# Attention rows stored by token and gathered by the experts, instead of scattered into expert order

## The chip, the cores and the metric

The kernel runs on one core of a Trainium2 chip. The metric is the device time of one execution in microseconds (us); the median of three runs stands for the kernel. A profile is one further execution, with the hardware profiler on.

## The reference

Sliding-window attention with a distance bias feeds a top-1 mixture of experts. All is float32.

```python
# attention: B, H, S, D = 8, 8, 576, 64; window 128
scores = scale * q @ k.T + bias[h]            # bias: -slope(h) * distance
mask   = (rel >= 0) & (rel < 128)
attn   = softmax(where(mask, scores, -1e9))
x      = (attn @ v) as (B*S, H*D)              # N = 4608 tokens, 512 wide
# experts: E = 8, F = 1024
logits     = x @ w_gate                        # (N, 8)
expert_idx = argmax(logits, axis=1)
gate_w     = softmax(logits)[expert_idx]
y[n]       = relu(x[n] @ w1[expert_idx[n]]) @ w2[expert_idx[n]]
out        = gate_w[:, None] * y
```

## The kernel before

**Attention stage.** The work is 32 units `u`: 8 sequences `b` times 4 pairs of heads `hp`. The order of instructions on each engine is written by hand (`manual_schedule`), so each engine executes in the order in which the Python code issues. One turn of the main loop (lines 902 to 949) issues `scores(u)` (TensorE, L641, with the exponentials on ScalarE, L648), `values(u - 1)` (TensorE, L674, then copies L681 and L682 on ScalarE and an addition L683 on VectorE), `factors(u)` (VectorE multiplies the exponentials by a table, L654 and L659), `totals(u - 1)` (TensorE, L695), and then a share of the routing of the sequence before.

**Routing.** A sequence is four token tiles of 128 rows (even `b`) or five (odd `b`). Its routing is spread over four turns of the loop:

1. `logits_t` and `fold`: gate products and softmax denominators (L755, L716).
2. `gate` and `pick`: the logits per token and the chosen expert (L775 to L182).
3. `place` (two products with 0/1 matrices, L194 and L195, then L198, L203, L204 on VectorE, which give `slots`, each token's row number in expert order), `gate_exps`, and `row` for tiles 0 and 1 (four transposes, L806, and a multiplication on VectorE, L809, which makes the row `xs`).
4. `row` for the remaining two or three tiles, then `gate_weights` (L792, L793).

Turn four also queues the tiles as `unsent`; `send()` (L816) then lets GpSimd copy token number and gate weight into the row (L822) and scatter 128 rows of 528 floats with one indirect DMA (L138) into `x_rows`, a DRAM tensor with a region of N rows per expert. Two or three tiles are sent per turn.

**Buffers of PSUM.** Seven kinds of intermediate share one pool, `ps_m`, with three buffers under the one name `m`, handed out in turn: two for each `values`, two for `logits_t`, one for `fold`, one or two for `gate`, one for `place`, one for each `row`. A request waits until whoever reads the tile three requests back has finished with it.

**Between the stages.** `last_tasks` (L857) routes the last sequence and runs layer 1 of the first two tiles of expert 0 (the `early` group, read at L853 from the rows of the first six sequences). Rows that no token filled are cleared by scatters of a zero row (`clear`, L147), after `number_all_free` (L214) found them. `extras` (L405) lists the tiles beyond four per expert.

**Expert stage.** Each expert has a full group of four tiles, computed by seven half-size products instead of eight (`seven1`, `seven2`, products at L1048); after each expert but the first there is a group of one further tile (L507, L518). `gather` (L1144) clears free rows and loads the group's rows with plain DMAs of SyncE (L1151); `turn` transposes them (L498); `tokens` (L476) takes token numbers and gate weights out of the rows; `send_out` (L465) scatters results to `out` from GpSimd. Weights of an expert (w1 and w2, 2 MB each) are loaded one group ahead into two buffers each (L239, L246).

Of the kernel before, what the change touches and what calls it, by code (L numbers as in the profile page):

```python
# [15 lines left out]
P = 128  # L16
# [5 lines left out]
def kernel(  # L22
# [81 lines left out]
    tok_i = iota("tok", [P, NT], [[P, NT]], 0, 1, whole=True)  # L104

# [12 lines left out]
    x_d = nc.dram_tensor("x_rows", (E * N, RW), F32, kind="Internal").ap()  # L118
    x_tok = nc.dram_tensor("x_by_token", (NT, P, RW), F32, kind="Internal").ap()
    zero_row = consts.tile([P, RW], F32, name="zero_row")  # L120
    soon.append(lambda: nc.gpsimd.memset(zero_row[:], 0.0))
    soon.append(lambda: nc.gpsimd.memset(zero_row.bitcast(I32)[:, Dm : Dm + 1], 2 * N))


    EJ = 2
    free_rows = rte.tile([P, E, NJ], I32, name="free_rows")
    early_free = rte.tile([P, EJ], I32, name="early_free")
    late_free = rte.tile([P, EJ], I32, name="late_free")

    def number_free(out, tmp, count, tail, start, end):  # L130

        nc.vector.tensor_tensor(tmp, count, tail, op=ALU.add)
        nc.vector.tensor_scalar(out, tmp, scalar1=float(end), scalar2=float(E * N), op0=ALU.is_ge, op1=ALU.mult)
        nc.vector.tensor_tensor(tmp, tmp, out, op=ALU.add)
        nc.vector.tensor_tensor(out, tmp, start, op=ALU.add)

    def to_x_rows(row, numbers, apart=True):
        ins = nc.gpsimd.indirect_dma_start(  # L138
            out=x_d[:, :], out_offset=bass.IndirectOffsetOnAxis(ap=numbers, axis=0),
            in_=row, in_offset=None, bounds_check=E * N - 1, oob_is_err=False,  # L140
        )
        ins = getattr(ins, "ins", ins)
        if apart:
            tc.declare_no_dep(ins, group="rows_in", reason="disjoint rows")
            tc.add_to_no_dep_group("rows_in", ins)

    def clear(rows, apart=True):  # L147
        for j in range(rows.shape[1]):
            to_x_rows(zero_row[:], rows[:, j : j + 1], apart)
# [37 lines left out]
    def place(tiles, tmp_pool, ps, name):  # L187
# [17 lines left out]
        if tiles[-1] == NT - 1:  # L205
            nc.vector.tensor_sub(cnt[:], rk[:, :, GT], region[:])
        elif t0 + n == early_end:
            nc.vector.tensor_copy(early_n[:], rk[:, 0, GT:])
            number_free(
                early_free[:], tmp_pool.tile([P, EJ], F32, name="free", bufs=1)[:], early_n[:].to_broadcast([P, EJ]),  # L210
                tail[:, :EJ], region[:, 0:1].to_broadcast([P, EJ]), EJ * P,
            )

    def number_all_free(tmp_pool):  # L214

        tmp = tmp_pool.tile([P, E, NJ], F32, name="free", bufs=1)
        late = tmp_pool.tile([P, 1], F32, name="late", bufs=1)
        nc.vector.tensor_scalar_max(late[:], cnt[:, 0:1], float(EJ * P))
        number_free(
            late_free[:], tmp[:, 0, :EJ], late[:].to_broadcast([P, EJ]), tail[:, :EJ],  # L220
            region[:, 0:1].to_broadcast([P, EJ]), CAP,
        )
        number_free(
            free_rows[:], tmp[:], cnt[:].unsqueeze(2).to_broadcast([P, E, NJ]),
            tail[:, None, :].to_broadcast([P, E, NJ]), region[:].unsqueeze(2).to_broadcast([P, E, NJ]), CAP,
        )

    def scatter(t, row):
        to_x_rows(row, slots[:, t : t + 1])
# [26 lines left out]
    def shifted():  # L256
        with tc.tile_pool(name="bias", bufs=1) as b_pool, \
# [44 lines left out]
            for t in range(NT):  # L302
# [83 lines left out]
                nc.vector.tensor_copy(xs.bitcast(I32)[:, Dm : Dm + 1], tok_i[:, t : t + 1])  # L386
                nc.vector.reciprocal(xs[:, Dm + 1 : Dm + 2], gw[:])
                nc.sync.dma_start(x_tok[t], xs[:])
# [87 lines left out]
    def tokens(g):  # L476

        n = g["n"]
        bits = g["xg"].bitcast(I32)[:, :n, Dm]
        si = plain.tile([P, NJ], I32, name="si", bufs=2)  # L480
        g["si"], g["gw"] = si, plain.tile([P, NJ], F32, name="gw", bufs=2)
        if "mask" in g:
            nc.vector.tensor_tensor(si[:, :n], bits, g["mask"][:, 0, :], op=ALU.bitwise_and)
            nc.vector.tensor_tensor(si[:, :n], si[:, :n], g["mask"][:, 1, :], op=ALU.bitwise_or)
        else:
            nc.vector.tensor_copy(si[:, :n], bits)
        nc.vector.tensor_copy(g["gw"][:, :n], g["xg"][:, :n, Dm + 1])
# [66 lines left out]
    with tc.tile_pool(name="tab", bufs=1) as tab, \  # L554
# [50 lines left out]
        later.append(lambda: nc.vector.tensor_copy(ends.bitcast(I32)[:, :, 0], tok_i[:]))  # L605
# [184 lines left out]
        def gate_weights(ts):  # L790
            tt = slice(ts[0], ts[-1] + 1)
            nc.vector.tensor_scalar_add(gsum[:, tt], gsum[:, tt], 1e-9)  # L792
            nc.vector.reciprocal(ends[:, tt, 1], gsum[:, tt])  # L793
# [21 lines left out]

        def send():  # L816
            ts, i = unsent.pop(0)
            t = ts[i]
            xs = xs_of[t]
            if i % RG == 0:  # L820
                n = min(RG, len(ts) - i)
                nc.gpsimd.tensor_copy(xs.bitcast(I32)[:, :n, Dm:], ends.bitcast(I32)[:, t : t + n, :])  # L822
            scatter(t, xs[:, i % RG, :])
            if t + 1 == early_end:
                early.update(early_group())
# [5 lines left out]

        def routing_of(b):
# [4 lines left out]
                [lambda: place(ts, rows, ps_m, "m"), lambda: gate_exps(ts)],  # L837
            ]

        def rows_of(b):  # L840
            ts = tiles_of(b)
            parts = [
                [lambda: row(ts, 0), lambda: row(ts, 1)],
                [lambda i=i: row(ts, i) for i in range(2, len(ts))] + [lambda: gate_weights(ts)],
            ]
            parts[1].append(lambda: unsent.extend((ts, i) for i in range(len(ts))))
            return parts


        def early_group():  # L850
            clear(early_free, False)
            g = dict(n=EJ, apart=True, xg=plain.tile([P, EJ, RW], F32, name="xg2"))
            nc.sync.dma_start(g["xg"][:], x_d[: EJ * P, :].rearrange("(j p) r -> p j r", p=P))  # L853
# [3 lines left out]
        def last_tasks():  # L857
# [3 lines left out]
            turns.append(lambda: tokens(g))  # L861
# [17 lines left out]
            unsent.extend((ts, i) for i in range(len(ts)))  # L879
            row(ts, 1)  # L880
            for i in range(2, len(ts)):
                some(1)
                send()
                row(ts, i)
            run([send, send])
            number_all_free(rows)
            clear(late_free)
            some(FB - 6)
            extras(tab.tile([P, H, 2 * C], F32, name="fac").rearrange("p h c -> p (h c)"))
# [12 lines left out]
        for u in range(NU + 1):  # L902
# [32 lines left out]
            if u > 0:  # L935
                totals(u - 1)
            some = routing[:1]
# [7 lines left out]
            for _ in range(min(len(unsent), 3 if len(unsent) > 6 else 2)):  # L945
                send()
# [197 lines left out]
    def gather(g):  # L1144
        n = g["n"]
        if g.get("e", 0) > 0:
            clear(free_rows[:, g["e"], :])
        xg = g["xg"] = pools["x"].tile([P, NJ, RW], F32, name="xg")
        src = g["rows"]().rearrange("(j p) r -> p j r", p=P)
        for j0, j1 in ((0, 2), (2, n)) if n > 2 else ((0, n),):  # L1150
            nc.sync.dma_start(xg[:, j0:j1, :], src[:, j0:j1, :])  # L1151
# [16 lines left out]
    def rows_of_x(x, of=xr):  # L1168
        r0 = nc.sync.value_load(of[0:1, x], min_val=0, max_val=E * N - P)
        return x_d[bass.ds(r0, P), :]  # L1170
# [8 lines left out]

    def experts():  # L1180
        groups = []
        for e in range(E):

            j0 = EJ if e == 0 else 0
            groups.append(dict(
                n=NJ - j0, e=e, rows=lambda r=e * N + j0 * P, n=NJ - j0: x_d[r : r + n * P, :], apart=True,
            ))
            if e > 0:
                x = slice(e - 1, e)
                groups.append(dict(  # L1190
                    n=1, of=lambda x=x: of_x(x), rows=lambda x=x: rows_of_x(x), mask=xmasks[:, :, x], apart=True,
                ))
# [6 lines left out]
        turns = [lambda: turn(g, range(g["n"])), lambda: tokens(g)]  # L1199
        layer2(early, EJ - 1, bank(2), zx[:], between=turns)  # L1200
        for i, g in enumerate(groups):
            after = groups[i + 1 : i + 3] + [None, None]
            full = [a for a in after if a is not None and a["n"] == NJ and "w1s" not in a]
            if after[1] is not None:
                gather(after[1])
            if after[0] is not None:
                after[0]["w2"] = load_w2(after[0]["src"][1])
            if g["n"] == NJ:
# [4 lines left out]
                if i == 1:  # L1213
                    what_is_left()
                seven1(g, 1, order, two_banks(3), temps(), {})
# [7 lines left out]
            if after[0] is not None:  # L1223
                turn(after[0], range(after[0]["n"]))
                tokens(after[0])
# [9 lines left out]
            else:  # L1235
                plain_layer2(g, ahead=[is_there_more] if i == len(groups) - 1 else ())

# [10 lines left out]
    def plain_group(g):  # L1248
# [4 lines left out]
        tokens(g)  # L1253
# [4 lines left out]
    def one_tile(i, of, first_row, masks):  # L1258
# [3 lines left out]
        plain_group(dict(  # L1262
            n=1, of=lambda: of_x(x, of), rows=lambda: rows_of_x(x, first_row), mask=mk, apart=False,
        ))

    def all_again():

        shifted()
        with tc.tile_pool(name="again", bufs=1) as again:
            with tc.For_i(0, NT, 1) as i:  # L1270
                xs = again.tile([P, RW], F32, name="xs")
                sl = again.tile([P, 1], I32, name="sl")
                nc.sync.dma_start(xs[:], x_tok[bass.ds(i, 1)].rearrange("o p r -> (o p) r"))
                nc.vector.tensor_copy(sl[:], slots[:, bass.ds(i, 1)])
                to_x_rows(xs[:], sl[:], False)
# [66 lines left out]
```

## Time and profile before

| what | value |
|---|---|
| median of 3 runs | 703.37 us (703.27 to 705.43) |
| the profiled execution, its own time | 718.1 us |
| its span, first to last instruction | 716.3 us |
| TensorE busy | 686.2 us, 96% of the span |
| VectorE busy | 345.6 us, 48% |
| GpSimd busy | 122.0 us, 17%, in 147 instructions |
| mean granted TensorE clock | 0.990 |

The attention stage takes the first 180 us or so, the part between the stages some 35 us, the expert stage the rest. A busy share is an average over these; TensorE's instructions overlap, so its busy time does not mean that it runs at its peak. In a timeline, the columns are start, busy time, engine, line, operation, tiles written and read, shape, count, and in brackets the idle time before and what ended it.

### The profile page before, as it was taken

To read this page: it belongs to the slowest core of one execution; us is meant where nothing else is said; L and a number is where in the kernel's file an instruction comes from. 1 tells how busy PE (TensorE), PEld (TensorE's weight loads), DVE (VectorE), ACT (ScalarE), POOL (GpSimd) and SP (SyncE) were. 2 spreads that over 40 slices of the span, in tenths; PEclk is the share of its full clock that TensorE was granted. 3 is DMA by queue.
4 is the path that set the end of the run, shared out by engine and by line. 5 is a ranking of instruction groups with operands and counts; after the bars stand their busy time and mean duration, and the time that the engine had idled before them with its cause. 6 is when DMAs were issued, how large, how long until landed. Compare 5 with 4: busy or idle time off the path is not lost.

```text
span 716.3 us, 13671 instructions
## 1 busy us (share of the span) xinstructions
PE 686.2 (96%) x5662; PEld 560.5 (78%) x5662; DVE 345.6 (48%) x706; ACT 215.7 (30%) x543; POOL 122.0 (17%) x147
## 2 busy tenths in 40 slices
PE   6999999999899999999999999999999999999992
PEld 5877676877667588978897887889788888878880
DVE  4677666676663263436335533634463453426300
ACT  5656454654311121222131212112131221222120
POOL 2020323024343020121022002202200220110020
PEclk9999999999999999999999999999999999999997
DMA  9966799742236635255363617534463836272010
GB/s 278 282 213 186 239 299 300 212 163 78 92 107 237 235 118 208 79 221 178 134 202 143 235 52 279 187 138 153 153 190 122 272 112 226 72 272 83 1 60 4
DMA packets 52722, 122.03 MB, mean 170 GB/s; under 512 B 7185, under 2 KB 7185, under 8 KB 52656
## 3 DMA queue, kind: packets, MB, share of 16 engines
q1 hardware_dynamic: 43568, 101.78, 43.6%
q0 software_dynamic: 8560, 19.32, 7.1%
q8 instruction: 45, 0.74, 0.4%
q14 instruction: 21, 0.17, 0.1%
q10 hardware_dynamic: 528, 0.02, 0.0%
HBM read 101.79 MB, written 28.61 MB: 182 GB/s over the span
## 4 chain that ended last, share of the span: by engine, by line
PE 70%; issue 11%; DVE 3%; POOL 1%; ACT 0%; POOLq 0%; DVEq 0%
PE b L1048 17%; PE a L1048 12%; PE c L1048 12%; PE a L518 6%; PE m L674 3%; PE b L507 3%; PE a L507 3%; PE sp L641 2%; PE m L507 2%; PE c L507 2%; PE m L806 1%; PE sm L695 1%; PE tp L498 1%; PE c L518 1%; PE sp L518 1%
## 5 line engine op out<-in xcount | busy, mean ns | idle before, releaser
L466 POOL DMA_INDIRECT out_dram<-zo,si x28 | 29.6, 1059 | 292.8 <-ACT zo L1118 288.5
L648 ACT ACTIVATE e<-sp 128x384 f32<-128x384 f32 x128 | 55.9, 491 | 49.4 <-PE sp L641 28.1
L674 PE MATMUL m<-probs,v_sb 64*64 64x192 f32 (+2 forms) x1152 | 63.9, 318 | 6.2 <-issue 4.4
L674 PEld LDWEIGHTS m<-probs,v_sb 64*64 64x64 f32 x1152 | 54.3, 137 | 15.9 <-issue 9.8
L641 PE MATMUL sp<-q_sb,k_sb 64*64 64x192 f32 (+2 forms) x1152 | 57.1, 325 | 6.4 <-DMA k_sb<-in_kT_dram 5.1
L641 PEld LDWEIGHTS sp<-q_sb,k_sb 64*64 64x64 f32 x1152 | 47.7, 138 | 17.1 <-issue 6.8
L518 PE MATMUL a<-w,h 128*128 128x512 f32 x128 | 56.3, 592 | 0.0
L1118 ACT ACTIVATE zo<-zo,gw 128x256 f32<-128x256 f32 x42 | 19.1, 501 | 119.4 <-DVE zo L1129 78.2
L1048 PE MATMUL a<-xgT,w 128*128 128x256 f32 x224 | 53.0, 379 | 0.0
L1048 PE MATMUL b<-xTs,w1s 128*128 128x256 f32 x224 | 52.9, 379 | 0.0
L1048 PE MATMUL a<-w,h_sb 128*128 128x256 f32 x224 | 50.6, 379 | 0.0
L1048 PE MATMUL b<-w2s,hs 128*128 128x256 f32 x224 | 50.6, 379 | 0.0
L1048 PEld LDWEIGHTS a<-xgT,w 128*128 128x128 f32 x224 | 42.5, 190 | 8.7 <-issue 3.3
L1048 PEld LDWEIGHTS b<-xTs,w1s 128*128 128x128 f32 x224 | 42.6, 190 | 5.8
L1048 PEld LDWEIGHTS b<-w2s,hs 128*128 128x128 f32 x224 | 42.6, 190 | 5.8
L1048 PEld LDWEIGHTS a<-w,h_sb 128*128 128x128 f32 x224 | 42.0, 190 | 5.4
L518 PEld LDWEIGHTS a<-w,h 128*128 128x128 f32 x128 | 23.7, 190 | 26.8 <-issue 26.8
L654 DVE TENSOR_TENSOR probs<-e,fac 128x1152 f32<-128x1152 f32 x32 | 43.3, 1352 | 2.4 <-ACT e L648 2.4
L138 POOL DMA_INDIRECT x_rows<-xs,slots x36 | 38.4, 1066 | 14.7 <-POOL xs L822 6.1
L1078 DVE TENSOR_TENSOR u<-b,p 128x512 f32<-128x512 f32 x14 | 9.7, 692 | 56.3 <-PE b L1048 35.3
L1082 ACT ACTIVATE h_sb<-h_sb 128x512 f32<-128x512 f32 x14 | 8.8, 630 | 84.3 <-DVE h_sb L1081 84.3
L683 DVE TENSOR_TENSOR xT<-xT,m 128x128 f32<-128x128 f32 x32 | 9.1, 284 | 48.7 <-ACT xT L682 47.3
(248 smaller groups left out, 1152.2 us busy)
## 6 DMA issues: line engine op xcount, KB each, us to landing
w<-in_moe_w_dram SPq DMA_DIRECT2D x28, 2048.0 KB
q_sb<-in_qT_dram SPq DMA_DIRECT2D x32, 288.0 KB
k_sb<-in_kT_dram SPq DMA_DIRECT2D x32, 288.0 KB
xg<-x_rows SPq DMA_DIRECT2D x16, 528.0 KB
v_sb<-in_v_dram SPq DMA_DIRECT2D x24, 256.0 KB
w<-in_moe_w_dram SPq DMA_DIRECT2D x8, 512.0 KB
v_sb<-in_v_dram SPq DMA_DIRECT2D x24, 128.0 KB
xg<-x_rows SPq DMA_DIRECT2D x7, 264.0 KB
```

What stands on the lines that cost most here:

```text
L138: ins = nc.gpsimd.indirect_dma_start(out=x_d[:, :], out_offset=bass.IndirectOffsetOnAxis(ap=numbers, axis=0), in_=row, in_offset=None, bou ...
L466: ins = nc.gpsimd.indirect_dma_start(out=out[:, :], out_offset=bass.IndirectOffsetOnAxis(ap=g["si"][:, j : j + 1], axis=0), in_=row, in_of ...
L507: nc.tensor.matmul(ps[:, :n], lhsT=g["w1"][:, db, fb * P : (fb + 1) * P], rhs=g["xT"][:, db, :n], start=(db == 0), stop=(db == DB - 1),)
L518: nc.tensor.matmul(ps[:], lhsT=g["h"][:, fb, j * P : (j + 1) * P], rhs=g["w2"][:, fb, :], start=(fb == 0), stop=(fb == FB - 1),)
L641: nc.tensor.matmul(sp_banks[2 * par + s][r * HALF : (r + 1) * HALF, c : c + n], lhsT=k_sb[u][head, k0 : k0 + HALF], rhs=q_sb[u][head, q0 : ...
L648: nc.scalar.activation(exps[u][:, c], sp_banks[s][:, : W // 2], AF.Exp, scale=D ** -0.5)
L654: nc.vector.tensor_tensor(to[:, :, : 3 * C].rearrange("p a (j c) -> p a j c", c=C), e[:, :, : 3 * C].rearrange("p a (j c) -> p a j c", c=C ...
L674: nc.tensor.matmul(xp[r][par * HALF : (par + 1) * HALF, q0 : q0 + n], lhsT=v_sb[b][keys, i, h * D : (h + 1) * D], rhs=probs[u][keys, par, ...
L683: nc.vector.tensor_add(to[:, QB0:QA], to[:, QB0:QA], xp[1][:, : QA - QB0])
L1048: nc.tensor.matmul(out_of[:, i, :], lhsT=lhs(i, k), rhs=rhs(k), start=(first and i == 0 and k == 0), stop=(k == nk - 1), skip_group_check= ...
L1078: nc.vector.tensor_add(u2[:], bb, p1[:])
L1118: nc.scalar.activation(o[:, th, dh, i, :], src[:, i, :], AF.Copy, scale=g["gw"][:, j : j + 1])
```

## The change

Rows are written by token number into `x_rows` (now N rows) with plain DMAs of SyncE, at most two tiles each. Which token stands in which place of an expert's first four tiles is found on chip: for each sequence `in_tiles` splits `slots` into lane (low 7 bits) and tile, and builds two 0/1 matrices on VectorE, the second multiplied by token number plus one; `hold` multiplies them on TensorE and adds the result to `held`. `where_held` turns `held` into token numbers to read from and to write to. `gather` then reads each tile by an indirect DMA of GpSimd. Tokens beyond the first four tiles are listed in DRAM by 36 scatters of 128 token numbers, issued after expert 0's group; SyncE reads seven lists of 128 back at group 2, and two VectorE operations mask them. The clearing scatters, `number_free` and `number_all_free` go. The one-tile groups move one expert later: none after expert 1, two after expert 7.

```diff
-    x_d = nc.dram_tensor("x_rows", (E * N, RW), F32, kind="Internal").ap()
+    x_d = nc.dram_tensor("x_rows", (N, RW), F32, kind="Internal").ap()
+    t_d = nc.dram_tensor("tokens_by_expert", (E * N, 1), I32, kind="Internal").ap()
...
+    def where_held(t_in, t_out, n, tmp_pool):
+        none = tmp_pool.tile([P, E * NJ], F32, name="none", bufs=1)[:, :n]
+        nc.vector.tensor_scalar(none, held[:, :n], scalar1=0.5, scalar2=float(2 * N), op0=ALU.is_lt, op1=ALU.mult)
+        nc.vector.tensor_scalar(t_in, held[:, :n], scalar1=-1.0, scalar2=0.0, op0=ALU.add, op1=ALU.max)
+        nc.vector.scalar_tensor_tensor(t_out, in0=held[:, :n], scalar=-1.0, in1=none, op0=ALU.add, op1=ALU.add)
...
+    def in_tiles(tiles, tmp_pool):
...
+        nc.vector.tensor_single_scalar(parts_i[:, 0, :n], slots[:, tt], P - 1, op=ALU.bitwise_and)
+        nc.vector.tensor_single_scalar(parts_i[:, 1, :n], slots[:, tt], 7, op=ALU.logical_shift_right)
+        nc.vector.tensor_copy(parts[:, :, :n], parts_i[:, :, :n])
+        nc.vector.tensor_tensor(
+            at_tile[:, :n], cols.rearrange("p e j -> p (e j)")[:, None, :].to_broadcast([P, n, E * NJ]),
+            parts[:, 1, :n].unsqueeze(2).to_broadcast([P, n, E * NJ]), op=ALU.is_equal,
+        )
+        nc.vector.tensor_tensor(
+            at_tile[:, :n], at_tile[:, :n], tok1[:, tt].unsqueeze(2).to_broadcast([P, n, E * NJ]), op=ALU.mult,
+        )
+        nc.vector.tensor_tensor(
+            at_lane[:, :n], lane[:, None, :].to_broadcast([P, n, P]),
+            parts[:, 0, :n].unsqueeze(2).to_broadcast([P, n, P]), op=ALU.is_equal,
+        )
...
+    def hold(tiles, at_lane, at_tile, m):
+        n = len(tiles)
+        for i in range(n):
+            nc.tensor.matmul(
+                m[:, : E * NJ], lhsT=at_lane[:, i, :], rhs=at_tile[:, i, :], start=(i == 0), stop=(i == n - 1),
             )
+        nc.vector.tensor_add(held[:], held[:], m[:, : E * NJ])
...
         def send():
             ts, i = unsent.pop(0)
...
-            scatter(t, xs[:, i % RG, :])
+            nc.sync.dma_start(
+                x_d[t * P : (t + n) * P, :].rearrange("(i p) r -> p i r", p=P), xs_of[t][:, :n, :],
+            )
...
+        def finish_routing(b):
+            gate_exps(tiles_of(b))
+            inside[b] = in_tiles(tiles_of(b), rows)
...
-                [lambda: place(ts, rows, ps_m, "m"), lambda: gate_exps(ts)],
+                [lambda: place(ts, rows, ps_m, "m"), lambda: finish_routing(b)],
...
-                [lambda i=i: row(ts, i) for i in range(2, len(ts))] + [lambda: gate_weights(ts)],
+                [lambda i=i: row(ts, i) for i in range(2, len(ts))] + [
+                    lambda: gate_weights(ts), lambda: end_rows(ts, nc.gpsimd), lambda: hold_of(b),
+                ],
...
             for i in range(2, len(ts)):
                 some(1)
-                send()
                 row(ts, i)
-            run([send, send])
-            number_all_free(rows)
-            clear(late_free)
+            end_rows(ts, nc.vector)
+            run([send] * len(unsent))
+            inside[NB - 1] = in_tiles(ts, rows)
             some(FB - 6)
+            hold_of(NB - 1)
+            where_held(held_in[:], held_out[:], E * NJ, rows)
             extras(tab.tile([P, H, 2 * C], F32, name="fac").rearrange("p h c -> p (h c)"))
...
     def gather(g):
-        n = g["n"]
-        if g.get("e", 0) > 0:
-            clear(free_rows[:, g["e"], :])
         xg = g["xg"] = pools["x"].tile([P, NJ, RW], F32, name="xg")
-        src = g["rows"]().rearrange("(j p) r -> p j r", p=P)
-        for j0, j1 in ((0, 2), (2, n)) if n > 2 else ((0, n),):
-            nc.sync.dma_start(xg[:, j0:j1, :], src[:, j0:j1, :])
+        for j in range(g["n"]):
+            read_row(xg[:, j, :], g["ti"][:, j : j + 1])
...
+            for x0 in {0: (), 1: (), E - 1: (E - 3, E - 2)}.get(e, (e - 2,)):
...
+            if i == 2:
+                for x in range(XU):
+                    tokens_of_x(x_read[:, x : x + 1], slice(x, x + 1))
...
+                if i == 2:
+                    mask_tokens(x_in[:], x_out[:], x_read[:], xmasks[:, :, :XU])
...
+            if i == 0:
+                for t in range(NT):
+                    scatter_tokens(slots[:, t : t + 1], tok_i[:, t : t + 1])
```

`read_row` is one indirect DMA of GpSimd that reads 128 rows of `x_rows` by number; `end_rows` copies the gate weights into the rows of a sequence (GpSimd in the loop, VectorE for the last sequence) and queues them; `weights_of` takes the place of `tokens`, with one copy instead of two; `hold_of` calls `hold` with a tile `m` of `ps_m`. The loop now runs every pending `send` right after `totals(u - 1)`.

## The prediction

> **What bounds the kernel now.** I read the table of stages first, then the list of waits, then the timelines of single engines.
>
> ```profile
> 50.00:100.00 50.00, 47.51 (x855) 35.80 (x848) 33.87 (x88) 25.59 (x76) 14.12 (x19) 1.00 0.74 234
> 100.00:150.00 50.00, 47.20 (x836) 36.83 (x836) 31.74 (x83) 26.90 (x79) 11.73 (x15) 0.97 0.85 267
> 300.00:350.00 50.00, 50.00 (x259) 42.07 (x258) 23.31 (x36) 11.84 (x25) 8.98 (x9) 1.00 0.62 215
> ```
>
> Columns after the stretch: busy us of TensorE, its weight loads, VectorE, ScalarE, GpSimd, then clock, DMA share, GB/s. TensorE sets the pace in both stages. In the expert stage it is never idle (the timeline has no gap over 0.2 us from 215 to 702 us), so nothing that shortens gathers or clears there can show. In the attention stage it is busy 94% and VectorE 65%. The list of waits says who holds TensorE up: from 40 to 215 us it names VectorE's rows `xs` (0.8 us, matmuls) and no load but one of 0.3 us. GpSimd's longest waits are for others (124 us for the gate weights): its scatters are on nobody's path by name.
>
> The edge that decides is in turn three, seen on TensorE and then on VectorE:
>
> ```profile
> 87.21 1.57 PE L641 MATMUL sp<-q_sb,k_sb 64*64 64x192 f32 x35
> 88.56 0.34 PE L674 MATMUL m<-probs,v_sb 64*64 64x192 f32 x2
> 88.63 1.52 PE L674 MATMUL m<-probs,v_sb 64*64 64x192 f32 x34
> ```
>
> ```profile
> 87.46 0.20 DVE L198 TENSOR_TENSOR sc<-m,sel 128x32 f32<-128x32 f32 x1
> 87.69 0.19 DVE L203 TENSOR_REDUCE slots<-sc 128x4 int32<-128x32 f32 x1
> 87.80 0.17 DVE L204 COPY sel<-pre 128x8 f32<-128x8 f32 x1
> 87.87 1.29 DVE L809 TENSOR_TENSOR xs<-m,rs_all 128x512 f32<-128x512 f32 x2
> ```
>
> The second half of `values` needs the buffer `m` of row 0, three requests back. VectorE reads it out by 87.87 + 0.65 = 88.52; the `values` start at 88.56. There is 0.1 us to spare. Where four small operations (L132 to L135, 0.7 us) came in between, for sequence 5, TensorE already stood:
>
> ```profile
> 158.43 0.34 PE L674 MATMUL m<-probs,v_sb 64*64 64x192 f32 x2
> 159.23 1.52 PE L674 MATMUL m<-probs,v_sb 64*64 64x192 f32 x32 [0.47 <-DVE xs L809]
> ```
>
> [...] 284 to 290 ns (L683, 128), 650 to 692 (L809, 512). [...] the trace has 0.98 us of GpSimd per indirect DMA and 1.28 from one to the next. [...]
>
> **Part 1: `in_tiles`, turn three.** VectorE executes in order, and these six operations come after `place` and before row 0. Four tiles: 0.16 + 0.16 + 0.17 (small ones, as L792 or L204), 0.29 + 0.29 (128 elements), 0.65 (512), and six gaps of 0.04: 1.96 us. Five tiles: 0.16 + 0.16 + 0.17 + 0.32 + 0.32 + 0.82 + 0.24 = 2.19. Queued behind them are `xs` of rows 0 and 1, and behind `xs` the second half of `values`: TensorE waits for nearly all of it. Sequences 0, 2, 4, 6: 4 x 1.86 = 7.4. Sequences 1 and 3, with 0.2 spare: 2 x 2.0 = 4.0. Sequence 5 loses `number_free` (0.7): 1.5. Sum **12.9 us**. Bounds: 9 (0.5 us more spare in each) to 16 (operations a quarter slower).
>
> **Part 2: `hold`, turn four.** A float32 product takes two passes; `place`'s two products took four, and the next transposes began 0.47 us after the first:
>
> ```profile
> 133.75 0.42 PE L194 MATMUL m<-pre,ones_sq 128*128 128x48 f32 x2
> 134.01 0.38 PE L195 MATMUL m<-sel,lt_strict 128*128 128x40 f32 x2
> 134.22 1.07 PE L806 MATMUL m<-ident,xT 128*128 128x128 f32 x8
> ```
>
> So 0.117 us a pass: 0.94 us for four tiles, 1.17 for five, plus about 0.17 of hand-over. It is bare TensorE time, 1.1 for each even sequence. With five tiles there is a wait too: three rows precede `hold`, so its buffer is that of row 2, which VectorE reads only after `factors`:
>
> ```profile
> 161.48 1.53 PE L806 MATMUL m<-ident,xT 128*128 128x128 f32 x12
> 162.94 1.57 PE L641 MATMUL sp<-q_sb,k_sb 64*64 64x192 f32 x35
> ```
>
> ```profile
> 162.71 0.55 DVE L659 TENSOR_TENSOR probs<-e,fac 128x384 f32<-128x384 f32 x1
> 163.18 1.88 DVE L809 TENSOR_TENSOR xs<-m,rs_all 128x512 f32<-128x512 f32 x3
> ```
>
> `scores` would start at 162.94; row 2 is free at 163.18 + 0.65 = 163.83: 0.9 us of standing, then 1.2. Four even ones 4 x 1.1 = 4.4, three odd ones 3 x 2.1 = 6.3: **10.7 us**; bounds 7 (no wait) to 13. The addition into `held` (0.2) runs beside `scores`.
>
> **Part 3: between the stages.** VectorE gets three copies (0.6), `in_tiles` (2.2), then `held` and `where_held` (0.2 + 0.6), and loses eight operations (1.8). The copies start after the last `xs` at 204.6, so the matrices are ready at 207.5, when layer 1 has just ended (207.2): wait 0.3, `hold` 1.2: **1.5 us**. The gather of expert 0's last two tiles starts after `where_held`, about 209.5; with 2 x 1.28 and an estimated 3 us to land it is there by 215, and its transposes run at 221. `extras` ends two us later, near 216, with no reader before 237. `weights_of` saves 0.2 before layer 1 of the early group, whose own gather is issued 10 us sooner than needed.
>
> **Part 4: covered, at nothing.** SyncE's `send`s stand behind a turn's loads and ahead of the next turn's, which are four turns ahead; cover gone, 1 or 2 us. Gathers on GpSimd (39 x 1.28 us, a group ahead) replace 32 clears and 36 row scatters. The 36 late scatters take 46 us of GpSimd from 253 to 299; the sends of expert 1's group come at 298, the lists are read from 301, masked near 315, and first transposed near 325. If they come late, VectorE waits at the mask with the sums of group 2 behind it. Weights with no one-tile group between experts 1 and 2 have 48 us for 2 MB. The same products in another order: 0.
>
> **The sum.** 12.9 + 10.7 + 1.5 - 0.2 = 24.9 us on the profiled execution's 718.1. That is 14.7 above the median. I find most of it in the first turns of the cycles: between starts of `scores` they took 6.6, 7.5, 6.7, 9.9, 6.0 and 6.9 us where others take about 5.2, 12.4 in all, with TensorE trickling for no wait that the profile names. All six have row scatters landing; the one before any scatter took 4.2. The expert stage cannot give 14 us, being full, so I take these stretches to be mostly of the profiled execution, and add the sum to the median: 703.4 + 24.9 = 728; I take **727**.
>
> **Rivals.** *Relief.* The trickling is in unprofiled runs too and comes from GpSimd's scatters: 12.4 us go, 728 - 12.4 = 716. For: it stands only where scatters land. Against: the excess of the profiled run, and that the same bytes are still written. Chance 0.16. *Faster.* Relief, and the added VectorE work hides as well, because VectorE is idle 1.6 us later in turn three: left are 7 of part 2 and 1.3 of part 3, giving 703.4 - 12.4 + 8.3 = 699. It decides where the cost per sequence falls under 12.4 / 8 = 1.5 us; I count 3.1. Against: order on VectorE is fixed. Chance 0.06. *Slow lists.* The scatters of four bytes run late, group 2 stands some 8 us: 736. Chance 0.08. *Clock.* New standing of 2 us makes the throttle act, as it did for 3.4 us at half speed after the trickle at 121 to 125 us: seven times 1.7 us, 740. Chance 0.08. *No effect* of all this within 0.3%: 0.02. The forecast keeps 0.60.
>
> The range leaves out the fast rival, the clock and a part of the slow lists: 711 to 738. About 0.3% is what a measurement here can tell from no change.
>
> **Right or wrong.** In the profile after: L674 waits on VectorE `xs` about 2 us in every third turn; the new products take 0.9 to 1.2 us and odd ones wait 0.9; group 2 has no gap; the expert stage keeps its length; the trickling remains. If third turns keep 5.1 us, part 1 is wrong; if first turns drop to 5.2 and the medians fall with them, the relief was real.

## The result, and the profile after

| | median, us | range |
|---|---|---|
| before, 4 runs | 704.40 | 703.27 to 705.75 |
| after, 4 runs | 739.83 | 736.92 to 743.22 |

The ratio is **1.0504** (95% interval 1.0451 to 1.0556). The direction was foretold, the size was not: the forecast was 727, its range ended at 738. The profiled execution of after took 740.76 us, with a span of 739.0 and a mean clock of 0.983.

The stages first, with the same columns as before (stretch; busy us of TensorE, its weight loads, VectorE, ScalarE, GpSimd; clock, DMA share, GB/s):

```profile
50.00:100.00 50.00, 46.20 (x881) 37.92 (x873) 36.39 (x98) 26.60 (x78) 0.85 (x5) 1.00 0.71 218
100.00:150.00 50.00, 46.18 (x911) 38.09 (x914) 35.71 (x99) 27.62 (x80) 1.21 (x7) 1.00 0.92 279
300.00:350.00 50.00, 38.87 (x175) 33.79 (x174) 20.17 (x27) 7.11 (x14) 29.00 (x26) 0.91 0.48 101
```

In the attention stage TensorE has lost 1.0 to 1.3 us of 50, GpSimd is nearly free. The surprise is the third line: in the expert stage, where TensorE was never idle, 11 us of 50 are gone and the clock has dropped. The list of waits (who waited, for what; total, times, longest) names the causes:

```profile
PE b L1072 <- DVE u L1102: 11.1, 1, 11.1
PE m L683 <- DVE xs L818: 9.9, 7, 2.0
PE sp L650 <- DMA k_sb<-in_kT_dram: 5.1, 1, 5.1
PE tp L507 <- DMA xg<-x_rows,held_in: 4.5, 1, 4.5
PE m L243 <- DVE xs L818: 2.7, 3, 0.9
```

The load of `k_sb` was there before. The other four are new, or larger. Turn three, on TensorE and then on VectorE, for sequence 2:

```profile
92.84 1.57 PE L650 MATMUL sp<-q_sb,k_sb 64*64 64x192 f32 x35
94.19 0.34 PE L683 MATMUL m<-probs,v_sb 64*64 64x192 f32 x2
94.21 0.22 PE L650 MATMUL sp<-q_sb,k_sb 64*64 64x64 f32 x1
94.36 0.34 PE L683 MATMUL m<-probs,v_sb 64*64 64x192 f32 x2
95.90 1.52 PE L683 MATMUL m<-probs,v_sb 64*64 64x192 f32 x32 [1.21 <-DVE xs L818]
```

```profile
93.54 0.17 DVE L224 TENSOR_SCALAR parts_i<-slots 128x4 int32<-128x4 int32 x1
...
94.56 0.68 DVE L234 TENSOR_TENSOR at_lane<-lane,parts 128x512 f32<-128x512 f32 x1
95.16 1.28 DVE L818 TENSOR_TENSOR xs<-m,rs_all 128x512 f32<-128x512 f32 x2
```

`in_tiles` stands between `slots` and the first row, from 93.54 to 95.16, and TensorE waits 1.21 us for that row's buffer. Turn four of an odd sequence, in which `hold` waits for the buffer of row 2 and then takes TensorE's time:

```profile
166.88 1.53 PE L815 MATMUL m<-ident,xT 128*128 128x128 f32 x12
169.32 1.30 PE L243 MATMUL m<-at_tile,at_lane 128*128 128x32 f32 x10 [0.91 <-DVE xs L818]
170.55 1.57 PE L650 MATMUL sp<-q_sb,k_sb 64*64 64x192 f32 x35
```

What the forecast had no term for: GpSimd between the stages, and VectorE at group 2.

```profile
225.90 1.03 POOL L482 DMA_INDIRECT out_dram<-e,early_out  x1 [29.86 <-ACT e L531]
227.24 1.04 POOL L152 DMA_INDIRECT xg<-x_rows,held_in  x1 [0.31 <-issue]
228.59 1.00 POOL L152 DMA_INDIRECT xg<-x_rows,held_in  x1 [0.30 <-issue]
```

```profile
334.05 0.72 DVE L1039 TENSOR_TENSOR hs<-h_sb,hs 128x512 f32<-128x512 f32 x1
346.76 0.17 DVE L1174 TENSOR_TENSOR x_in<-x_read,xmasks 128x7 int32<-128x7 int32 x1 [11.98 <-DMA x_read<-tokens_by_expert]
```

```profile
334.77 1.89 PE L1072 MATMUL c<-xTs,w1s 128*128 128x256 f32 x8
347.79 2.50 PE L1072 MATMUL b<-xTs,w1s 128*128 128x256 f32 x5 [11.13 <-DVE u L1102]
```

The gather of expert 0's last tiles could have gone soon after `hold` and `where_held` (218.6), but stands in GpSimd's order behind a `send_out` that waits for ScalarE until 225.90. And VectorE idles 12 us at the mask for the lists, with the sums of group 2 behind it, for which TensorE waits. Why the lists are late is seen on GpSimd and SyncE, and in the view of the list tensor:

```profile
331.32 1.14 POOL L140 DMA_INDIRECT tokens_by_expert<-tok_i,slots  x1 [0.30 <-DMA tokens_by_expert<-tok_i,slots]
338.23 6.90 SPq L1194 DMA_DIRECT2D x_read<-tokens_by_expert  x7
```

```profile
L140 POOL DMA_INDIRECT tokens_by_expert<-tok_i,slots x36: 977/982/1933, 271.4 to 331.3; - x36
...
  DMA tokens_by_expert<-tok_i,slots: 13.1, 8
...
DMA to landing us min/median/max: 1.9/8.2/18.3
```

The 36 scatters run from 271.4 to 332.5, 61 us; in 13.1 of them GpSimd itself waits for earlier ones to land, which takes 8.2 us in the median.

### The profile page after: what moved, and what is told of

It reads as the page before. It is cut to its first block, busy times and chain, and to the rows that moved or that the text cites. A ratio compares the mean times of both kernels' runs of the same rounds, so it can differ in the third digit from the quotient of the medians.

```text
span 739.0 us, 13847 instructions
## 1 busy us (share of the span) xinstructions
PE 692.3 (94%) x5734; PEld 570.3 (77%) x5734; DVE 355.8 (48%) x740; ACT 216.5 (29%) x543; POOL 129.4 (18%) x152
## 4 chain that ended last, share of the span: by engine, by line
PE 58%; issue 24%; DVE 8%; POOL 5%; DMA 3%; SPq 1%; POOLq 0%; ACT 0%; DVEq 0%
PE b L1072 14%; PE a L1072 9%; PE c L1072 9%; PE m L683 6%; PE a L527 5%; PE sp L650 4%; POOL tokens_by_expert L140 3%; PE sm L704 3%; DVE probs L663 2%; DMA tokens_by_expert<-tok_i,slots 2%; PE b L516 2%; PE a L516 2%; POOL xg L152 1%; PE m L815 1%; PE c L516 1%
## 5 line engine op out<-in xcount | busy, mean ns | idle before, releaser
L482 POOL DMA_INDIRECT out_dram<-zo,held_out x28 | 29.8, 1064 | 235.8 <-ACT zo L1142 230.9
L683 PE MATMUL m<-probs,v_sb 64*64 64x192 f32 (+2 forms) x1152 | 60.0, 324 | 10.7 <-DVE xs L818 9.9
L683 PEld LDWEIGHTS m<-probs,v_sb 64*64 64x64 f32 x1152 | 54.1, 141 | 16.7 <-DVE xs L818 12.4
L1072 PE MATMUL b<-xTs,w1s 128*128 128x256 f32 x224 | 54.8, 389 | 11.1 <-DVE u L1102 11.1
L650 PE MATMUL sp<-q_sb,k_sb 64*64 64x192 f32 (+2 forms) x1152 | 54.9, 326 | 7.3 <-DMA k_sb<-in_kT_dram 5.1
L140 POOL DMA_INDIRECT tokens_by_expert<-tok_i,slots x36 | 39.8, 1104 | 21.6 <-DMA tokens_by_expert<-tok_i,slots 13.1
L152 POOL DMA_INDIRECT xg<-x_rows,held_in x30 | 32.5, 1083 | 9.1 <-issue 9.1
```

The lines of the kernel that those rows point to most:

```text
L140: ins = nc.gpsimd.indirect_dma_start(out=t_d[:, :], out_offset=bass.IndirectOffsetOnAxis(ap=numbers, axis=0), in_=toks, in_offset=None, bo ...
L152: nc.gpsimd.indirect_dma_start(out=to, out_offset=None, in_=x_d[:n, :], in_offset=bass.IndirectOffsetOnAxis(ap=tok, axis=0), bounds_check= ...
L482: ins = nc.gpsimd.indirect_dma_start(out=out[:, :], out_offset=bass.IndirectOffsetOnAxis(ap=g["si"][:, j : j + 1], axis=0), in_=row, in_of ...
L650: nc.tensor.matmul(sp_banks[2 * par + s][r * HALF : (r + 1) * HALF, c : c + n], lhsT=k_sb[u][head, k0 : k0 + HALF], rhs=q_sb[u][head, q0 : ...
L683: nc.tensor.matmul(xp[r][par * HALF : (par + 1) * HALF, q0 : q0 + n], lhsT=v_sb[b][keys, i, h * D : (h + 1) * D], rhs=probs[u][keys, par, ...
L1072: nc.tensor.matmul(out_of[:, i, :], lhsT=lhs(i, k), rhs=rhs(k), start=(first and i == 0 and k == 0), stop=(k == nk - 1), skip_group_check= ...
```

## The experiments

Each group of kernels was run beside before on one chip. Before took 703.9, 704.4 and 705.1 us on three chips, and 717.6, 717.9 and 719.2 on three others; this turned out to matter. Each chip was used for one group, so it isn't shown whether the chip or its state at the time makes the difference; "kind of chip" below means only what before took there. After itself took 739.8, 736.9 and 739.6 us in three groups, so a difference from after across groups is uncertain by some 3 us.

**1. The four terms, one at a time** (before 703.93; the last one on another chip, before 704.41).

`tiles_after_rows`: `in_tiles` behind rows 0 and 1 on VectorE.

```diff
-            inside[b] = in_tiles(tiles_of(b), rows)
...
-                [lambda: row(ts, 0), lambda: row(ts, 1)],
+                [lambda: row(ts, 0), lambda: row(ts, 1), lambda: inside.update({b: in_tiles(ts, rows)})],
```

> The kernel after, with in_tiles issued behind rows 0 and 1 instead of ahead of them; the same instructions. Theory (TensorE waits for xs only because six operations stand in front of it): the seven waits of 9.9 us in all fall to what before had, 0.8, and the half-speed stretch at 188 us goes: 739.8 - 9.1 - 3 = 728, between 726 and 732. Rival (VectorE is simply full in these turns): the wait moves to the next factors and values, gain under 4 us, 736 or more.

Measured 731.47 us, 8.4 under after, within the theory's range; L683 no longer waits for `xs`. Part 1 is the place of `in_tiles` in VectorE's order. The gain isn't the sum of its waits alone: the half speed at 188 us is gone too, and the wait for the lists grew from 11.1 to 12.9 us.

`hold_first`: `hold` ahead of rows 2 to 4.

```diff
-                [lambda i=i: row(ts, i) for i in range(2, len(ts))] + [
-                    lambda: gate_weights(ts), lambda: end_rows(ts, nc.gpsimd), lambda: hold_of(b),
-                ],
+                [lambda: hold_of(b)] + [lambda i=i: row(ts, i) for i in range(2, len(ts))] + [
+                    lambda: gate_weights(ts), lambda: end_rows(ts, nc.gpsimd),
+                ],
```

> The kernel after, with hold issued ahead of rows 2 to 4 instead of behind them. Theory (with five tiles hold waits for the buffer of row 2): the three waits of 0.9 us go, 737, between 736 and 738.5. Rival (row 4 now waits for the addition into held, in the buffer that hold took): 739 to 741.

Measured 739.56: in the rival's range, but without the rival's wait, since no row waits for the addition in the trace. The three waits (2.7 us) are gone; the wait for the lists grew from 11.1 to 14.7 us. So the number doesn't decide.

`gather_first`: the gather of expert 0's last tiles straight after `where_held`, ahead of the `send_out`.

```diff
             where_held(held_in[:], held_out[:], E * NJ, rows)
+            early["next"] = plain.tile([P, EJ, RW], F32, name="xg2")
+            for j in range(EJ):
+                read_row(early["next"][:, j, :], held_in[:, EJ + j : EJ + j + 1])
...
-        gather(g)
+        g["xg"] = early["next"]
```

> The kernel after, with the gather of expert 0's last two tiles issued right after where_held, ahead of the first result send on GpSimd. Theory (the gather stood behind that send, which waits for ScalarE, and then competed with 4 MB of weights): the 4.5 us gap at the transposes goes, with 1.4 us of half speed: 734, between 733 and 736. Rival (an indirect gather takes 7 us to land wherever it stands): the gap keeps 2 us or more, 737 to 740.

Measured 734.93, 4.9 under after (2.0 under its lowest median); the wait of 4.5 us is gone, and the one for the lists grew to 14.1.

In these three runs all that is saved early still passes through the lists. The scatters start 10.4, 6.8 and 8.3 us sooner than in after (261.0, 264.6, 263.1 for 271.4), but the mask runs only 8.7, 3.3 and 5.5 us sooner, and the profiled spans are shorter by just about that: 7.8, 2.7 and 4.5 us. In each, the 36 scatters took 62 to 64 us.

`lists_later`: lists read and masked at expert 3's group.

```diff
-            for x0 in {0: (), 1: (), E - 1: (E - 3, E - 2)}.get(e, (e - 2,)):
+            for x0 in {0: (), 1: (), 2: (), E - 1: (E - 4, E - 3, E - 2)}.get(e, (e - 3,)):
...
-            if i == 2:
+            if i == 3:
```

> The change with the lists read and masked one full group later (at expert 3's group instead of expert 2's), and the one-tile groups one expert later again: none after experts 1 and 2, three after expert 7. The scatters stay where they are. Theory (group 2's wait of 11.1 us is the lists', and the half clock after it costs some 3 us more): 739.8 - 11 to 14 = 726 to 729. Rival (the scatters themselves, or what is waiting elsewhere, take it back): 735 or more.

Measured 731.05, 8.8 under after, where 11 to 14 were expected. The 11.1 us wait is gone, but another comes out from under it: the rows of expert 3's group are gathered by GpSimd behind the 36 scatters, and TensorE waits for them from 341.6 and 345.7 us. These are the list of waits' lines for them, with the known 4.3 us of expert 0 in the first:

```profile
PE tp L507 <- DMA xg<-x_rows,held_in: 6.4, 2, 4.3
PE b L507 <- DMA xg<-x_rows,held_in: 1.1, 1, 1.1
```

**2. The scatters spread over the attention stage.**

```diff
                 unsent.append((ts, i))
+            for t in ts:
+                scatter_tokens(slots[:, t : t + 1], tok_i[:, t : t + 1])
```

> The kernel after, with the 36 scatters of token numbers issued sequence by sequence in the attention loop, where GpSimd is nearly idle. Theory (the lists come late because GpSimd starts them only after expert 0 and then waits for its own landings): the 11.1 us gap of group 2 goes, and with it the half-speed stretch behind it (some 1.7 us): 739.8 - 12.8 = 727, between 724 and 730. Rival (scatters landing in the attention loop make TensorE trickle, as in the first turns of before): less than 5 us gained, 735 or more, and first turns of 6 us and more.

Measured 759.52 (ratio 1.0821, 1.0749 to 1.0894). The theory is missed. The rival had the sign right (735 or more, TensorE held up), but neither the size nor the place: the first turns keep 4.2 to 4.9 us, and five second turns take 7.0 to 12.5 instead of 5.5. The wait for the lists is gone, but TensorE stands for nothing that the trace names, though before takes 703.9 on this chip:

```profile
PE sp L650 <- issue: 14.0, 8, 5.2
PE m L683 <- issue: 8.8, 4, 4.6
```

That is 23 us; the mean clock fell to 0.972. Other transfers are slow at the same time: from 114 to 122 us, around the stand of 4.6 us, packets of 2 to 4 KB took 497 ns in the mean, against 121 in after in that stretch. That TensorE stood because of them isn't shown, as it waits for no load there. Whether its instructions, which come by DMA too (the two queues `instruction` on after's page, 68 packets with 0.93 MB), were late wasn't tested.

**3. Matrices and storage apart.** `before_matrices` puts `in_tiles` and `hold` of the diff into before, at the same places, and leaves scatters and clears as they were:

```diff
-                [lambda: place(ts, rows, ps_m, "m"), lambda: gate_exps(ts)],
+                [lambda: place(ts, rows, ps_m, "m"), lambda: finish_routing(b)],
...
-                [lambda i=i: row(ts, i) for i in range(2, len(ts))] + [lambda: gate_weights(ts)],
+                [lambda i=i: row(ts, i) for i in range(2, len(ts))] + [lambda: gate_weights(ts), lambda: hold_of(b)],
```

`before_plain_rows` changes the storing and leaves out the expert order: the experts get other rows than their own.

```diff
-            scatter(t, xs[:, i % RG, :])
+            place0 = t // NJ % E * N + (t % NJ + t // (E * NJ) * NJ) * P
+            nc.sync.dma_start(x_d[place0 : place0 + P, :], xs[:, i % RG, :])
```

> The kernel before, with its rows still scattered by GpSimd and its clears, and with in_tiles and hold added at the places that they have in the change; nobody reads their result. Theory (the matrices cost TensorE what the trace of the change shows, 9.1 us of waits for xs in turn three, 10.0 us in turn four, 1.3 between the stages): 704 + 20 = 724, range 720 to 728. Rival (part of what the change costs in the attention stage is of the new storage, not of the matrices): below 718.

> The kernel before with each row tile written by a plain transfer of SyncE to a fixed place instead of GpSimd's scatter; the experts so get other rows than their own, the amount of work is the same. Theory of the prediction (the slow first turns of before are mostly of its profiled execution): the median stays within 702 to 705, while its profile loses the slow turns and its own time falls by 10 us or more. Rival (the scatters disturb TensorE in every execution): 686 to 698.

Beside 704.41: matrices 729.24, plain rows 701.31 (ratio 0.9948, 0.9931 to 0.9965). So the matrices cost 24.8 us. That is 1.2 us above the expected range, and 4.7 more than the 20.1 that after's waits and products come to (9.1 + 10.0 + 1.0). Of these, 0.9 is in this trace itself, whose waits for `xs` are 10.8 us: `number_free` is still there in sequence 5. The clock can be the rest: its median over the runs is 0.991 for before and 0.985 here, and 0.006 of 729 us is 4.4, an estimate. The row scatters cost 3.1 us on this chip. That is 0.7 us more than the expected range allows, but far from the rival's; the profile has no slow first turns (4.2 to 4.8 us from one start of `scores` to the next), and its own time is 700.0. But `before_matrices`, which scatters its rows on the same chip, has none in its profile either (4.2 to 4.3).

**4. Together.** `four_later` joins the four edits of group 1. `five` also issues the gather of expert 3's rows ahead of the scatters. `five_bf16` splits the token number into tile and place, both exact in bfloat16, and multiplies in one pass.

```diff
             if i == 0:
+                gather(groups[3])
                 for t in range(NT):
```

```diff
-        at_tile = tmp_pool.tile([P, GT, E * NJ], F32, name="at_tile", bufs=1)
+        at_tile = tmp_pool.tile([P, GT, 2, E * NJ], mybir.dt.bfloat16, name="at_tile", bufs=1)
...
-                m[:, : E * NJ], lhsT=at_lane[:, i, :], rhs=at_tile[:, i, :], start=(i == 0), stop=(i == n - 1),
+                m[:, : 2 * E * NJ], lhsT=at_lane[:, i, :], rhs=at_tile[:, i].rearrange("p a e -> p (a e)"), start=(i == 0), stop=(i == n - 1),
```

> Four edits of the change together: in_tiles after rows 0 and 1, hold ahead of the last rows, the gather of expert 0's last two tiles straight after where_held, lists one full group later. Theory (the costs add): 739.8 - 8.4 - 2.7 - 4.9 - 12 = 712, range 708 to 716; what is left over before is then TensorE's own time for hold, some 8 us. Rival (the waits overlap or move on): 718 or more. A version under 703 would beat both.

> The four edits of four_later, and the gather of expert 3's rows is issued ahead of the 36 late scatters on GpSimd instead of behind them. In the trace of four_later TensorE waits 5.3 + 1.7 + 0.4 us for these rows and then has 10.2 us of half clock. Theory (both are of the scatters' place in GpSimd's order): 715.3 - 7.5 - 0 to 4 = 704 to 708. Rival (rows are late because the four-byte transfers hold the DMA engines, whatever the order): 712 or more.

> As five, with the 0/1 matrices and the numbers in bfloat16: the token number is split into its tile (1 to 36) and its place in the tile (0 to 127), both exact, so hold multiplies by 64 columns instead of 32, in one pass instead of two. Theory (what is left of the matrices' cost is TensorE's time for hold, 36 products of two passes of 0.117 us, 8.4 us): half of it goes, four us less than five, 700 to 704. Rival (a product of 64 columns in one pass takes as long as two of 32, or VectorE's one operation more takes it back): within 1 us of five.

`four_later` took 715.30 beside 704.41 (ratio 1.0142, 1.0107 to 1.0178), within its theory's range: 24.5 us of the 35.4 are undone. Its trace has 7.5 us of waits for expert 3's rows. The other two fell on a chip where before took 715.4 to 721.5, in all 27 runs. There `five` took 700.6 to 734.1 and `five_bf16` 703.7 to 733.9: too scattered to say anything of the expectations. TensorE stood for "issue" between 264 and 291 us, while the scatters ran.

**5. Fewer numbers written.** `five_few` and `bf16_few` give the scatters a number out of bounds for every token that already has its place in a first tile.

```diff
+        nc.vector.tensor_tensor(past, at_b, region_b, op=ALU.is_ge)
+        nc.vector.scalar_tensor_tensor(
+            far, in0=at_b, scalar=-float(NJ * P), in1=region_b, op0=ALU.add, op1=ALU.is_ge,
+        )
+        nc.vector.tensor_sub(past, past, far)
...
-                    scatter_tokens(slots[:, t : t + 1], tok_i[:, t : t + 1])
+                    scatter_tokens(late_slots[:, t : t + 1], tok_i[:, t : t + 1])
```

> As five, but the 36 late scatters get a number out of bounds for each token that already stands in one of the first four tiles of its expert, so that only the tokens beyond them are written: a few hundred of 4608. Two tenths of VectorE's extras more, and one plain transfer that fills the list tensor beforehand. Theory (the four-byte transfers themselves disturb TensorE while they land, on some chips): 700 to 706 whatever before takes, with a spread of under 6 us, and the scatters follow each other by 1.28 us without waits for their own landings. Rival (it is GpSimd's issuing of indirect transfers, not the traffic): 715 to 725 with the spread of five where before takes 718.

> As five_few, with the matrices in bfloat16 and one pass of 64 columns for each product. Theory: some 4 us under five_few, 697 to 702, which would be under before on every chip. Rival (VectorE's matrices are then late for hold, as they were in five_bf16 by 0.2 to 0.5 us a sequence): the same as five_few within 1.5 us.

> The changed kernel once more, to be read by what before takes on the same chip. Where before takes 704: 740 as the first time. Where before takes 718, theory (the row scatters' slow turns are real on such a chip, and the change has none): 740 too, so a ratio of 1.03 instead of 1.05. Rival (such a chip is slower in everything): 754, the same ratio of 1.05.

> Before with plain writes of rows instead of GpSimd's scatters, once more (the experts get other rows than their own). Where before takes 704: 701, as the first time. Where before takes 718, theory (the scatters make the slow turns): 701 to 704, a gain of 14 to 17. Rival (the chip is slower in everything): 715.

Beside 705.05: after 736.94 (1.0446, 1.0402 to 1.0490), plain rows 701.47 (0.9951), `five_few` 704.10 (0.9993, 0.9978 to 1.0009), `bf16_few` **701.06** (0.9944, 0.9924 to 0.9964). The scatters' landing fell from 8.2 to 2.7 us in the median and GpSimd no longer waits for it. So without the waits the change equals before here, and in bfloat16 it is 0.56% faster, as fast as before with plain rows. Its clock is higher too (0.9985 in the median of its runs, for 0.991), which by the estimate above is worth the whole gain. It lies 3 us under `five_few` where 4 were expected: a product takes one pass of 0.193 us for 64 columns, but VectorE's matrices and additions are now waited for (1.7 and 3.2 us). As before takes 705 here, this chip doesn't decide between the theory and the rival of `five_few`.

**6. The other kind of chip.** `bf16_spread` issues the scatters one after each product in the program.

```diff
             run(more.get(n, ()))
+            if late:
+                late.pop(0)()
```

> Before with plain writes of rows (the experts get other rows than their own), as twice before. Where before takes 704: 701. Where before takes 718, theory (the scatters make the slow turns): 701 to 704. Rival (such a chip is slower in everything): 715.

> bf16_few once more. Where before takes 704: 701, a ratio of 0.992 to 0.997, as the first time. Where before takes 718, theory (four-byte writes and row scatters are what such a chip is slow at, and hardly any are left): 698 to 706. Rival: 715.

> The changed kernel beside before. Where before takes 704: 737 to 740. Where before takes 718, theory (the change has no row scatters left, but 36 late ones, which hold the engines up there by about 1 us each): 740 + 20 to 36 = 760 to 776, a ratio of 1.06 to 1.08. Rival (only the relief counts): 740, a ratio of 1.03.

> As bf16_few, with one late scatter after each of the next 36 products of the expert stage (about 3 us apart) instead of all in a row. Where before takes 704: 701, a ratio of 0.992 to 0.998. Where before takes 718, theory A (the unbroken row of issues holds the engines up): 698 to 706. Theory B (each scatter costs its 1 us wherever it stands): 730 to 740.

Beside 719.21, plain rows took 700.97 (ratio 0.9737, 0.9699 to 0.9774): here the row scatters cost 18 us. `bf16_few` took 737.59 (1.0223, 1.0173 to 1.0273): its theory (698 to 706) and its rival (715) both fail, and so does the theory of `five_few`, that few numbers written make it fast on every chip. Beside 717.64, on one more chip, after took 739.56 (1.0278, 1.0237 to 1.0319), as the rival expected and against the theory (760 to 776), and `bf16_spread` 717.32 (0.9990, 0.9969 to 1.0010), between its two theories. It was no clean test: nothing makes GpSimd wait for a product, so it issued 19 scatters in a row all the same. Its trace still says something: in that first row (250 to 276 us) TensorE was busy 16.2 of 26 us, in a second row of 16 (316 to 337) for all of it, 26.98 of the 27 us from 310 on. So neither such a chip nor an unbroken row is enough by itself.

The same kernel, `bf16_few`, on the two kinds of chip; first the line of the stage table where before takes 705:

```profile
250.00:310.00 60.00, 60.00 (x288) 53.03 (x287) 37.51 (x58) 13.99 (x26) 45.87 (x42) 1.00 0.42 127
```

and where it takes 719, with a stretch of TensorE's timeline there:

```profile
250.00:310.00 60.00, 33.80 (x131) 27.12 (x131) 17.58 (x31) 6.37 (x11) 39.09 (x40) 0.77 0.18 56
```

```profile
290.91 0.27 PE L528 MATMUL a<-ident,xg 128*128 128x128 f32 x1 [2.53 <-issue]
293.71 0.37 PE L528 MATMUL b<-ident,xg 128*128 128x128 f32 x1 [2.53 <-issue]
296.51 0.37 PE L528 MATMUL b<-ident,xg 128*128 128x128 f32 x1 [2.42 <-issue]
```

While GpSimd issues scatters (254.6 to 301), TensorE, VectorE and ScalarE all do about half their work, and TensorE gets one matmul in 2.8 us. Within 4 us of the last scatter it ends (from 304.91 fifteen products follow one another). The DMA share is lower, not higher (0.18 for 0.42), so it isn't full DMA engines; in before's slow turn at 121 to 125 us the share was 0.98, so the two need not be the same effect. ScalarE idled 17.5 us for "issue" in one piece, and TensorE stood for "issue" too. What holds them is open, and so is why after, with its 36 scatters of all numbers, shows hardly any of it on such a chip (TensorE is busy all of 270 to 302 us). One difference is untested: in `five`, `five_bf16`, `bf16_few` and the first row of `bf16_spread`, all held up on such chips, the scatters follow four gathers of rows; in after and in that second row they follow a result.

## Why the prediction was right or wrong

**The base.** I put the 14.7 us above the median down to the profiled execution. That reason was wrong, and so was the 12.4: a first turn without trouble takes not 5.2 us but 4.2 to 4.8, as all three traces of plain rows show (the text has one of 4.2 itself), so the six cost some 18 us. The profiler isn't their cause, as `before_matrices` was profiled with its rows scattered and has none, on a chip where before takes 704. Where before takes 719, plain rows take 18 us away. That the profiled execution came from such a chip isn't recorded; its 718.1 us and these 18 fit. Taking 703.4 as the base, and no relief, still fitted the chips that the medians came from: there the relief is 3.1 to 3.6 us, not 12.4. The *Relief* rival holds where before takes 718, with after 2.8% slower instead of 5.0% on the one such chip tried.

**Part 1**, 12.9 us: measured 9.1 (waits of 9.9 less the 0.8 of before), at the lower bound of 9. Wrong was the sum of six durations. From start to start `in_tiles` takes 1.62 us for four tiles (93.54 to 95.16) and 1.81 for five, not 1.96 and 2.19, since the next operation starts before the end of one that it doesn't need (L225 at 93.62, L224 ends at 93.71). The single durations came as forecast, 0.29, 0.33, 0.68 and 0.82 us in the mean for 128, 160, 512 and 640 elements; before's trace had shown only those for 128 and 512. And the spare time was 0.4 us, not 0.1: in the lines above four products of `values` go ahead and 32 wait, while I measured up to the first.

**Part 2**, 10.7: measured 10.0. The 0.117 us a pass and the odd sequences' wait of 0.9 came as worked out.

**Part 3**, 1.5: measured 1.0 (`hold` from 216.75 to 217.78, without a wait in front), but "there by 215" for expert 0's last tiles failed. I gave the gather the time of its data and not its place in GpSimd's queue, behind a `send_out` that waits for ScalarE; the 3 us to land had no figure behind it either, and the median of after's gathers is 6.7. It cost a wait of 4.5 us, which is gone in `gather_first`.

**Part 4**, at nothing: this is the step that failed. I priced 36 scatters by the pitch of 1.28 us, 46 us, from rows of 2 KB. They took 61, mostly because the engine waits for its own four-byte transfers (13.1 us). The chain behind (landing, seven reads of SyncE in 6.9 us, the mask) took 14.3, against 16 forecast. And the need was set too late: not the transposes near 325, but the mask's place in VectorE's order, with TensorE dry from 336.7. The expert stage began 16.8 us later than before (268.9 for 252.1), so in the forecast's times that need is 319.9, 5 us behind the 315 for the mask; 15 us more for the scatters and 2 for their later start, less 2 for the shorter chain, leave about 10, and the sum behind the mask takes one more. The text named that queue ("VectorE waits at the mask") and *Slow lists* gave it 8 us; it took 11.1.

**The clock.** *Clock* expected every wait to cost. Half speed showed only at the longer stands (the trace's clock records: 3.4 us at 41, 6.8 at 188, 3.4 at 235, 10.2 at 341), none at the waits of 1.2 to 1.75 us. At 188 the 32 products took 2.83 us, for 1.52 in the lines above:

```profile
188.37 2.83 PE L683 MATMUL m<-probs,v_sb 64*64 64x192 f32 x32 [2.01 <-DVE xs L818]
```

The stretches last 3.41 us, or two or three times that (6.83, 10.24). Stands of 1.8 (at 41) and 2.0 us (at 188) were enough for a drop, but the same wait of 2.0 us in `hold_first` brought none; what decides isn't shown. By the mean clock of the runs, 0.991 before (median in groups 1 and 3) and 0.983 after, it cost about 0.008 x 740 = 5.9 us, an estimate. That the *Clock* rival's 740 is so near the measured 739.8 is chance: its term was twice as large, and the lists and the gather made up the rest.

**The sum again:** 704.4 + 9.1 + 10.0 + 1.0 - 0.2 (from the forecast, not measured) + 4.5 + 11.1 + 5.9 - 3.1 = 742.7, against 739.8. The 2.9 us too many may be overlap, which no run separates: half speed during a wait costs nothing (6.6 of the 10.2 us at 341 lie within the wait that ends at 347.8), and the plain rows' 3.1 holds a gain of clock too (0.994 for 0.991). So the forecast's three parts up to the expert stage were 25.1 us in text and 20.1 on the chip; what it missed are two places in queues (15.6 us) and the clock. That the three parts were 5.0 us too dear hid some of the miss, which was luck.

## What to carry to other kernels

When a transfer moves to another engine, write down the order of that engine's queue: a gather is as late as the `send_out` ahead of it (here 227.24 instead of 218.6), and an operation of 0.2 us on VectorE holds up all that follows it when its input is late (here for 12.0 us). Price a row of indirect transfers by their landings at that size (8.2 us in the median here), not by the pitch of larger ones (1.28 us). And where the profiled execution is 2% over the medians, run before again beside the change on several chips before deciding that it is the profiler: here the same kernel takes 704 us on some and 718 on others, and the best variant of the change gains on one kind and loses on the other.

## What was unexpected of the hardware

GpSimd's indirect transfers of four bytes land in 8.2 us in the median of after (18.3 at most) when 128 each follow one another, and in 2.7 in `five_few`, where few of the numbers are in bounds. Before takes 704 to 705 us on three of six chips and 718 to 719 on three; on one of the latter plain writes in place of 36 row scatters took 18 us away, and `bf16_few` took 36 us more than on a chip of the other kind, with TensorE, VectorE and ScalarE held up without a named wait while its late scatters were issued. A chain of six VectorE operations, some dependent and some not, takes 1.62 us where their durations and gaps sum to 1.96.
